# Feature-product weight operands made on GpSimd from blocks loaded once, the x operand made earlier, feature rows stored in pairs

## The chip, the cores and the metric

The kernel runs on one core of a Trainium2 chip. A core has a matrix engine (PE, with its own weight-load stream PEld), VectorE (DVE), ScalarE (ACT), GpSimd (POOL) and a sync engine (SP) that here issues nearly all DMAs, in program order, on one queue. The time is device time in microseconds; lower is better. All arithmetic is on 32-bit floats; a product of full precision is made from three matmuls on operands split into a high part (rounded to the matrix format `R`) and a low remainder.

## The reference

```python
def reference(A_x, A_wqkv, A_wo, ..., B_dft_seq_re, B_dft_seq_im, B_dft_hid_re, B_dft_hid_im, gate_w):
    x = A_x                                        # 1 x 2048 x 640
    g = sigmoid((x * gate_w).sum(-1, keepdims=True))
    q, k, v = split_heads(x @ A_wqkv)              # 32 heads of 20
    p = softmax(einsum("bhqd,bhkd->bhqk", q, k) * 20 ** -0.5)
    a = merge_heads(einsum("bhqk,bhkd->bhqd", p, v)) @ A_wo
    fa, fb = x @ B_dft_hid_re.T, x @ B_dft_hid_im.T   # features
    b = B_dft_seq_re @ fa - B_dft_seq_im @ fb
    return g * a + (1 - g) * b
```

## The kernel before

The work is one hand-ordered program; each engine gets its instructions in the order in which the Python code emits them.

**Projections.** First x is split and the first Q and K columns are made; then V in two halves of 320 columns (`v_pair`, two row tiles a call; each call first fills a V tile with ones on GpSimd, and two V tiles take turns). Then come 32 tiles of the remaining Q and K columns (`qk_pairs`, counted m = 0 to 31): 30 matmuls of 512 columns into two PSUM banks, ScalarE copies one bank out, VectorE adds the other, ScalarE rounds the sum and GpSimd subtracts to get the low part, and SP stores both to `qk_scr`. The low part of every later weight block `wt[c]` is also made on GpSimd (`fin`). Between the tiles PE makes the first score maxima (`run_s`): two steps a tile for m = 2 to 15, one for the others.

**Weight operands.** The features x @ W use a seven-product scheme (`FEATURE`): each product multiplies a sum or difference of two quarter blocks of x by a sum or difference of two quarter blocks of the DFT matrix. There are 14 sets of weight operands (7 products, 2 halves `hf`; 10 of the 14 have two terms). During the tiles `load_set(k)` loads the one or two blocks of a set (409,600 bytes each) into a `wide` tile, of which there are two; GpSimd adds (even m), ScalarE rounds, GpSimd subtracts (odd m), and SP stores the result to `w_scr` and then loads the next set over the same tile.

**Feature stage.** From m = 27 on `load_left(0)` makes the x operand of product 0, and `load_right` brings the stored weight sets back, 1.6 MB each. Then 56 cycles follow, c = 0 to 55, one feature unit u = c (`hid_pair`) in each, interleaved by the string `ORDER` with four steps of attention: scores (`L1052`), exponentials, the maxima of a coming head pair (`L191`) and, at the end of each cycle, a burst of 16 products with V (`L701`). An attention unit is 32 steps, or 8 cycles. A unit's maxima are transposed, stored to `m_scr` and loaded into rows of the q tile (`L240`); the scores of the next unit wait for them.

**Feature rows.** Each unit makes 2 x 128 rows of 320 columns. Rows that an earlier product has begun are added to. Those of products 2 and 4 (u = 16 to 23 and 32 to 39) are in DRAM (`a_scr`): `L489` loads them into one of three slots when the unit starts, GpSimd adds (`L509`), and they are stored eight steps after the unit ends. The fourth load of a product takes the slot of the first, and so waits until that slot's store has landed; SP waits with it, and so does all that follows on SP. Functions given to `at_step(i, ...)` are emitted at the start of attention step i; a unit u starts in step 4u + 1 and ends in step 4u + 3.

**After it** come the products along the sequence (seven products again, `dft_step`, `L782`), interleaved with attention in the same way until the end; `load_a` reads `a_scr` there.

## Time and profile before

| | us |
|---|---|
| median of 3 runs | 1894.74 (1892.43 to 1897.32) |
| the profiled execution | 1897.29 |
| its span | 1895.5 |
| PE busy | 1853.7 (98%) |
| DVE busy | 1453.8 (77%) |
| ACT busy | 1248.2 (66%) |
| POOL busy | 1293.3 (68%) |
| the 32 Q and K tiles | about 106 to 239 |
| the feature stage | about 239 to 607 |

Times in the profile count from the span's start. "A <- B" behind an idle time says that engine A was released by B. SPq is SP's queue of DMA issues. The granted clock (PEclk) is the share of its full rate that PE was given. A row of stretches ("A:B") gives the length, then each engine's busy time, the granted clock, the share of the DMA engines' time and the rate in GB/s.

### The profile page before, as it was taken

Reading aid. Unit: us, or ns where it says so; the run is one execution under the profiler, and the core shown is the slowest. Engines: PE = TensorE matmul, PEld = TensorE weight load, DVE = VectorE, ACT = ScalarE, POOL = GpSimd, SP = SyncE. Lnnn points to the kernel's source line nnn. Section 1 sums busy time; section 2 is a strip of 40 time slices with the busy share of each in tenths; the row PEclk is TensorE's granted clock in tenths of the full one; section 3 lists DMA queues with packets and bytes.
Section 4 is the critical chain, followed back from the end, with each engine's and each line's share of the span. In section 5 each row is a group of like instructions: output and inputs, shape, how many; then the busy total and the mean of one; then the engine's idle time right before and its main releaser. Section 6 shows DMA issues by size and latency. Waiting matters only on the chain. (4 is left out here: it accounts for less than half of the span.)

```text
span 1895.5 us, 45927 instructions
## 1 busy us (share of the span) xinstructions
PE 1853.7 (98%) x17917; PEld 1340.8 (71%) x17917; DVE 1453.8 (77%) x2420; ACT 1248.2 (66%) x2392; POOL 1293.3 (68%) x1092
## 2 busy tenths in 40 slices
PE   9999889989899999999999999999999999999998
PEld 8987657767566677777777777676767676766666
DVE  4156368878778888888888888888888888889953
ACT  4234357767567676767676767676767676777785
POOL 1267653465665999566688989968869988734444
PEclk9999989999999999999999999999999999999999
DMA  7769895677778676544657586747476756533214
GB/s 231 181 230 315 294 264 159 158 214 196 188 199 221 200 215 204 155 122 127 196 162 240 172 236 186 207 133 206 152 209 212 204 170 193 164 86 93 62 48 158
DMA packets 205820, 348.81 MB, mean 184 GB/s; under 512 B 54319, under 2 KB 124079, under 8 KB 205603
## 3 DMA queue, kind: packets, MB, share of 16 engines
q1 hardware_dynamic: 204643, 343.91, 62.3%
q0 software_dynamic: 960, 1.97, 0.6%
q8 instruction: 141, 2.31, 0.5%
q14 instruction: 76, 0.62, 0.1%
HBM read 264.34 MB, written 81.28 MB: 182 GB/s over the span
## 5 line engine op out<-in xcount | busy, mean ns | idle before, releaser
L193 DVE TENSOR_REDUCE mx<-ps 128x1 f32<-128x512 f32 x2048 | 1299.6, 685 | 255.1 <-PE ps L191 214.8
L1058 ACT ACTIVATE p<-ps 128x512 f32<-128x512 f32 x2048 | 1088.0, 598 | 456.8 <-PE ps L191 220.0
L191 PE MATMUL ps<-kst,qst 60*128 60x512 f32 x2048 | 781.4, 414 | 6.9 <-DVE mx L193 4.9
L1052 PE MATMUL ps<-qst,kst 62*128 62x512 f32 x2048 | 698.1, 416 | 13.1 <-DMA qst<-m_scr 13.1
L782 PE MATMUL yp<-x,part 64*128 64x320 f32 x5376 | 643.6, 306 | 0.0
L782 PEld LDWEIGHTS yp<-x,part 64*128 64x128 f32 x5376 | 581.4, 186 | 7.3
L1052 PEld LDWEIGHTS ps<-qst,kst 62*128 62x128 f32 x2048 | 334.4, 185 | 237.5 <-DVE mx L193 129.6
L701 PE MATMUL av<-p,v 128*21 128x512 f32 x4096 | 495.7, 599 | 0.0
L191 PEld LDWEIGHTS ps<-kst,qst 60*128 60x128 f32 x2048 | 370.8, 185 | 20.8 <-DVE mx L193 5.9
L131 POOL TENSOR_TENSOR part<-raw,part 128x1024 fp32r<-128x1024 f32 (+3 forms) x134 | 296.9, 2216 | 15.0 <-ACT part L128 4.8
L701 PEld LDWEIGHTS av<-p,v 128*21 128x21 f32 x4096 | 95.6, 100 | 209.4 <-issue 208.7
L496 PE MATMUL yp<-wb,x 64*128 64x320 f32 x1680 | 212.6, 312 | 7.7 <-POOL p L131 4.5
L130 POOL CAST part<-raw 128x1024 fp32r<-128x1024 f32 (+2 forms) x127 | 125.0, 984 | 134.1 <-PE yp L782 102.6
L643 POOL TENSOR_TENSOR raw<-raw,raw 128x1024 f32<-128x1024 f32 x78 | 188.0, 2411 | 34.2 <-DMA raw<-in_cdft 24.1
L496 PEld LDWEIGHTS yp<-wb,x 64*128 64x128 f32 x1680 | 183.7, 190 | 11.7 <-POOL p L131 4.8
L509 POOL TENSOR_TENSOR x<-x,raw 128x640 f32<-128x640 f32 x40 | 62.4, 1561 | 39.5 <-DVE raw L506 30.8
L131 POOL TENSOR_TENSOR x<-araw,x 128x320 fp32r<-128x320 f32 x96 | 83.8, 873 | 7.7
L853 PE MATMUL yp<-x,part 64*128 64x320 f32 x720 | 87.5, 309 | 0.0
L870 POOL TENSOR_TENSOR x<-x,m 128x320 f32<-128x320 f32 x30 | 26.2, 873 | 79.1 <-DVE m L865 68.2
L853 PEld LDWEIGHTS yp<-x,part 64*128 64x128 f32 x720 | 75.7, 185 | 2.7
L363 PE MATMUL yp<-x,part 64*128 64x512 f32 x480 | 66.0, 398 | 7.2 <-ACT p L369 6.0
L676 POOL TENSOR_TENSOR araw<-araw 128x320 f32<-128x320 f32 x80 | 69.9, 874 | 1.9 <-DMA araw<-a_scr 1.9
(101 smaller groups left out, 1364.7 us busy)
## 6 DMA issues: line engine op xcount, KB each, us to landing
raw<-in_cdft SPq DMA_DIRECT2D x188, 512.0 KB
araw<-a_scr SPq DMA_DIRECT2D x176, 160.0 KB
wb<-w_scr SPq DMA_DIRECT2D x28, 800.0 KB
qk_scr<-p SPq DMA_DIRECT2D x40, 512.0 KB
kst<-qk_scr SPq DMA_DIRECT2D x90, 160.0 KB
qst<-qk_scr SPq DMA_DIRECT2D x90, 160.0 KB
part<-in_xh SPq DMA_DIRECT2D x22, 512.0 KB
w_scr<-wb SPq DMA_DIRECT2D x14, 800.0 KB
```

The costliest lines, as they stand in the source:

```text
L130: e1.tensor_copy(dst1, src)
L131: e2.tensor_tensor(dst2, src, f32(dst1), op=ALU.subtract)
L191: pe.matmul(ps, q[b : b + KROWS, qt * P : (qt + 1) * P], k[b : b + KROWS, kc * 512 : (kc + 1) * 512], start=True, stop=True)
L193: return lambda: dve.tensor_reduce(mx[n][:, h, qt, kc : kc + 1], ps, axis=AX.X, op=ALU.max)
L496: pe.matmul(ps[z], lefts[n][a][r, d, k * P : k * P + P], rights[2 * n + hf][r, b, d], start=done_ == 0, stop=done_ == 3 * ND - 1)
L643: pool.tensor_tensor(raws[0], raws[0], raws[1], op=ALU.add if PRODUCTS[n][0][1][0] > 0 else ALU.subtract)
L676: pool.tensor_tensor(raws[0], raws[0], raws[1], op=ALU.add if PRODUCTS[n][1][1][0] > 0 else ALU.subtract)
L701: pe.matmul(av[32 * j : 32 * j + DH + 1, :], v[:, kt, h * (DH + 1) : (h + 1) * (DH + 1)], pp[qc][:, h, :], start=kt == 0, stop=kt == NS - 1)
L782: pe.matmul(yp[h][:, :HE], c[r, cz, cs], a[r, az], start=s == 0 and z == 0, stop=s == NS - 1 and z == 2)
L853: pe.matmul(yp[h][:, :HE], o[r, oz, d], wos[d, hf][r, wz], start=d == 0 and z == 0, stop=d == ND - 2 and z == 2)
L1052: pe.matmul(pt, k[b : b + KROWS + 2, kt * P : (kt + 1) * P], q[b : b + KROWS + 2, qc * 512 : (qc + 1) * 512], start=True, stop=True)
L1058: act.activation(pts[n, kt, qc][:, h], pt, AF.Exp, scale=float(DH) ** -0.5)
```

## The change

`load_weights(hf)` loads all four quarter blocks of one half at once, 1.6 MB in one DMA, into one `wide` tile: half 0 after the first call of the second V loop, half 1 after tile 8. `make_set` forms a set from those blocks with GpSimd alone: the sum (if there are two terms), the rounding that ScalarE did, and the subtraction. Three sets of half 0 are made during V, into pairs of `p` tiles; the other 11 go into the quarters of the second `wide` tile, one piece of work in each tile from m = 0 to 7 and from 9 to 22, now ahead of that tile's own low part. The high and the low part of a set are stored by a DMA each. The last tiles run in another order (for each of the four column groups t = 2, 3, 0, 1 the products n = 5, 6, 7), so that the x blocks of t = 2 are free after m = 22; the x operand is made from m = 23 on instead of from m = 28 on, and its loads and the `load_right` calls move up with it. The weight block of n = 7 is now finished after m = 19 and used at m = 22 (before: after m = 21, used at m = 25).

`a_scr` gets a layout in which the two row blocks of a unit lie side by side, so that a partition's row is 2,560 bytes in one piece and not two of 1,280. The load of the old rows is emitted four steps after the unit starts, and their store 11 steps after it ends and not 8. `load_a` and `load_a_early` follow the layout, and the first sequence operand uses a `raw` tile for its fourth block.

```diff
@@ -104,7 +104,7 @@
 
     qk_scr = dram.tile([2, 4, 2 * D, 512], F32, name="qk_scr")
     v_scr = dram.tile([NP, P, NS, VW], F32, name="v_scr")
-    a_scr = dram.tile([2, 2, NS, P, HE], F32, name="a_scr")
+    a_scr = dram.tile([2, 2, 2, 4, P, 2, HE], F32, name="a_scr")
     y_scr = dram.tile([NS, P, D], F32, name="y_scr")
     r_scr = dram.tile([NU, 4, 512], F32, name="r_scr")
     l_scr = dram.tile([NU, 4, 512], F32, name="l_scr")
@@ -322,7 +322,7 @@
 
         return finish
 
-    stores, halves = [], []
+    stores, halves, work_ = [], [], []
 
     def flush(keep=0):
         while len(stores) > keep:
@@ -369,6 +369,8 @@
         act.activation(raw, ps[0], AF.Copy)
         dve.tensor_tensor(raw, raw, ps[1], op=ALU.add)
         st = pair_tile()
+        if work_:
+            work_.pop(0)()
         split(st[:, 0].bitcast(R), st[:, 1].bitcast(R), raw, act, pool)
         store_qk(c, t, st, 1)
 
@@ -395,22 +397,23 @@
         flush(1)
 
 
-    def load_set(k):
-        _, terms, _, _ = FEATURE[k // 2]
-        w = wide.tile([P, 2, ND, BW], R, name="wb", bufs=2).rearrange("p z d c -> p (z d c)")
-        half = RW // 2
-        raws = [f32(w)[:, half * i : half * i + half] for i in range(2)]
-        for raw, (_, dh, ri) in zip(raws, terms):
-            sp.dma_start(raw, wr[ri, dh, k % 2])
-
+    def load_weights(hf):
+        w = f32(wide.tile([P, 2, ND, BW], R, name="wb", bufs=2)).rearrange("p z d c -> p (z d c)")
+        w = w[:, : 2 * RW].rearrange("p (b c) -> p b c", b=4)
+        sp.dma_start(w, wr[hf])
+        blocks_ = {(ri, dh): w[:, 2 * ri + dh] for ri in range(2) for dh in range(2)}
+        return [(2 * n + hf, [blocks_[ri, dh] for _, dh, ri in f[1]], f[1][-1][0]) for n, f in enumerate(FEATURE)]
+
+    def make_set(k, terms, sign, hi, lo):
         def add():
             if len(terms) > 1:
-                pool.tensor_tensor(raws[0], raws[0], raws[1], op=ALU.add if terms[1][0] > 0 else ALU.subtract)
+                pool.tensor_tensor(lo, terms[0], terms[1], op=ALU.add if sign > 0 else ALU.subtract)
 
         def finish():
-            split(w[:, 2 * half : 3 * half], w[:, 3 * half : 4 * half], raws[0], act, pool)
-            stores.append((w_scr[k].rearrange("z r (q c) -> (r q) z c", q=2),
-                           f32(w)[:, 2 * half : 4 * half].rearrange("p (z c) -> p z c", z=2)))
+            whole = lo if len(terms) > 1 else terms[0]
+            split(hi.bitcast(R), lo.bitcast(R), whole, pool, pool)
+            for z, part in enumerate((hi, lo)):
+                stores.append((w_scr[k, z].rearrange("r (q c) -> (r q) c", q=2), part))
 
         return add, finish
 
@@ -477,7 +480,7 @@
         ps = [new_y(z)[:, :HE] for z in range(2)]
         fresh = [(th, ri, hf, k) not in seen for _, th, ri in targets]
         seen.update((th, ri, hf, k) for _, th, ri in targets)
-        rows = [a_scr[ri, hf, th * HT + k : th * HT + HT : 4].rearrange("s p c -> p s c") for _, th, ri in targets]
+        rows = [a_scr[ri, hf, th, k] for _, th, ri in targets]
         olds = []
         for (_, th, ri), new, row in zip(targets, fresh, rows):
             old = None
@@ -486,7 +489,7 @@
             elif not new:
                 old = slots.pop(0)
                 slots.append(old)
-                sp.dma_start(old, row)
+                at_step(now[0] + 4, functools.partial(sp.dma_start, old, row))
             olds.append(old)
         done_ = 0
         for d in range(ND):
@@ -514,7 +517,7 @@
             if not new:
                 extras.append((now[0] + 3, functools.partial(add, sign, old)))
             if th != ri or ri == 0 and n == len(FEATURE) - 2 or ri == 1 and last:
-                at_step(now[0] + (4 if new else 8), functools.partial(sp.dma_start, row, m if new else old))
+                at_step(now[0] + (4 if new else 11), functools.partial(sp.dma_start, row, m if new else old))
         yield
 
     step = 0
@@ -561,37 +564,46 @@
         if s == 6:
             fin()
             fin = load_wqk(order[1], pool)
-        if s == 8:
-            sets = [load_set(0)]
+        if s == 0:
+            sets = load_weights(0)
+        if s in (4, 8, 12):
+            add, finish = make_set(*sets.pop(0), *(pair_tile().rearrange("p z c -> p (z c)")[:, : RW // 2] for _ in range(2)))
+            add(), finish()
         if s == 12:
             fin()
-    sets.append(load_set(1))
+    made_sets = f32(wide.tile([P, 2, ND, BW], R, name="wb", bufs=2)).rearrange("p z d c -> p (z d c)")
+    made_sets = made_sets[:, : 2 * RW].rearrange("p (q c) -> p q c", q=4)
+
+    def queue_sets():
+        for q, args in enumerate(sets):
+            work_.extend(make_set(*args, made_sets[:, q % 2 * 2], made_sets[:, q % 2 * 2 + 1]))
+        sets.clear()
+
+    queue_sets()
     free[0] = range(2, 5)
     fin = load_wqk(order[2], pool)
-    tiles = [(n, t) for n in range(6) for t in range(4)] + [(n, t) for t in (2, 3, 0, 1) for n in (6, 7)]
+    tiles = [(n, t) for n in range(5) for t in range(4)] + [(n, t) for t in (2, 3, 0, 1) for n in (5, 6, 7)]
     slabs = []
     for m, (n, t) in enumerate(tiles):
         qk_pairs(order[n], t, m)
         if m == 8:
             load_v(0)
-        if sets:
-            sets[0][m % 2]()
-            if m % 2:
-                sets.pop(0)
-            elif 2 <= m < 2 * SETS - 2:
-                flush()
-                sets.append(load_set(m // 2 + 1))
-        if n < 6 and t == 1:
+            sets = load_weights(1)
+            queue_sets()
+        if n < 5 and t == 1:
             fin()
             if n + 3 < len(order):
                 fin = load_wqk(order[n + 3], pool)
-        if m == 27:
+        if m == 19:
+            fin()
+        if m == 22:
             slabs = load_left(0, raw_stage)
-        if m in (28, 30):
+        if m in (24, 26):
             flush()
-            load_right((m - 28) // 2)
-        if m >= 27:
+            load_right((m - 24) // 2)
+        if slabs:
             slabs.pop(0)()
+    assert not work_
     free[0] = range(5)
     run_s(LEAD)
     flush()
@@ -648,11 +660,11 @@
     c_raws = []
 
     def load_c_first(g):
-        if not c_raws:
+        if g == 0:
             w = f32(wide.tile([P, 2, ND, BW], R, name="wb", bufs=2)).rearrange("p z d c -> p (z d c)")
-            c_raws.extend(w[:, 1024 * q : 1024 * q + 1024] for q in (0, 1, 2, 0))
+            c_raws.extend(w[:, 1024 * q : 1024 * q + 1024] for q in range(3))
         (_, th, ri), (sign, th2, ri2) = PRODUCTS[0][0]
-        raws = [c_raws.pop(0) for _ in range(2)]
+        raws = [c_raws.pop(0) if c_raws else raw_tile() for _ in range(2)]
         for raw, (half, part) in zip(raws, ((th, ri), (th2, ri2))):
             o = (2 * part + g % 2) * 1024
             sp.dma_start(raw, cdft[half * HT + g // 2, :, o : o + 1024])
@@ -668,7 +680,7 @@
         raws = []
         for _, ri, hf in PRODUCTS[n][1]:
             raws.append(apool[0].tile([P, HE], F32, name="araw", bufs=6))
-            sp.dma_start(raws[-1], a_scr[ri, hf, s])
+            sp.dma_start(raws[-1], a_scr[ri, hf, s // 8, s % 4, :, s // 4 % 2])
 
         def finish():
             a = a_tile(n % 2, s)
@@ -681,7 +693,7 @@
     def load_a_early(s0, s1):
         ((_, ri, hf),) = PRODUCTS[0][1]
         raw = f32(part_tile()).rearrange("p z c -> p (z c)")[:, : (s1 - s0) * HE].rearrange("p (s c) -> p s c", c=HE)
-        sp.dma_start(raw, a_scr[ri, hf, s0:s1].rearrange("s p c -> p s c"))
+        sp.dma_start(raw, a_scr[ri, hf, s0 // 8, :, :, s0 // 4 % 2].rearrange("k p c -> p k c"))
         for s in range(s0, s1):
             early.append((s, raw[:, s - s0]))
 
@@ -1012,7 +1024,7 @@
                 if slabs:
                     slabs.pop(0)()
                 if c in (HID - 9, HID - 7, HID - 5):
-                    for s in {9: (0, 8), 7: (4,), 5: (12,)}[HID - c]:
+                    for s in {9: (8, 0), 7: (4,), 5: (12,)}[HID - c]:
                         load_a_early(s, s + 4)
                 if HID - 8 <= c:
                     at_step(i + 2, make_a_early)
@@ -1197,7 +1209,7 @@
     wqk = w[:, : 2 * D].reshape(ND, P, 2 * ND, P).transpose(2, 1, 0, 3)
     xh = np.asarray(A_x)[0].reshape(2, 2, 512, 2, ND, 64).transpose(0, 3, 1, 5, 4, 2).reshape(2, 2, P, ND * 512)
     wr = np.stack([np.asarray(m) for m in (B_dft_hid_re, B_dft_hid_im)])
-    wr = wr.reshape(2, 2, HE, 2, ND, 64).transpose(0, 3, 1, 5, 4, 2).reshape(2, 2, 2, P, RW // 2)
+    wr = wr.reshape(2, 2, HE, 2, ND, 64).transpose(1, 0, 3, 5, 4, 2).reshape(2, 4, P, RW // 2).transpose(0, 2, 1, 3)
     wb = np.zeros((2, P, ND, BW), w.dtype)
     for hf in range(2):
         wb[hf, :, :, :HE] = w[:, 2 * D + hf * HE : 2 * D + (hf + 1) * HE].reshape(ND, P, HE).transpose(1, 0, 2)
```

SP around tile m = 8, where before sets are loaded over stored ones (`wb` is a `wide` tile, `in_wr` the DFT matrix, `w_scr` the finished sets, `in_wqk` a weight block, `v` the V tile of the first heads). Before, and then the change:

```order
L329 DMA qk_scr<-p 128x2x512
L329 DMA w_scr<-wb 128x2x800
L329 DMA qk_scr<-p 128x2x512
L404 DMA wb<-in_wr 128x800 x2
L300 DMA raw<-in_wqk 128x640
L329 DMA qk_scr<-p 128x2x512
L329 DMA w_scr<-wb 128x2x800
L329 DMA qk_scr<-p 128x2x512
L404 DMA wb<-in_wr 128x800
```

```order
L329 DMA w_scr<-wb 128x800 x2
L329 DMA qk_scr<-p 128x2x512
L559 DMA v<-v_scr 128x672
L403 DMA wb<-in_wr 128x3200
L329 DMA qk_scr<-p 128x2x512
L300 DMA raw<-in_wqk 128x640
L329 DMA qk_scr<-p 128x2x512
L329 DMA w_scr<-wb 128x800 x2
```

Between tiles there is no load of `in_wr` any more but this one; the two stores of a set stand where one stood.

GpSimd in the change from tile 17's weight block (`part_1980`, used from m = 21) past tile 19's (`part_2093`, used from m = 22), with the buffers' numbers; `p` is a tile's own low part:

```order
L131 TENSOR_TENSOR part_1980<-raw_1777,part_1980 128x640
L130 CAST wb_1027<-wb_1505 128x800
L131 TENSOR_TENSOR wb_1027<-wb_1505,wb_1027 128x800
L131 TENSOR_TENSOR p_2027<-p_2024,p_2027 128x512
L410 TENSOR_TENSOR wb_1027<-wb_1505 128x800
L131 TENSOR_TENSOR p_2088<-p_2024,p_2088 128x512
L131 TENSOR_TENSOR part_2093<-raw_1983,part_2093 128x640
L130 CAST wb_1027<-wb_1027 128x800
```

Each tile's `p` now stands behind the set's piece, the rounding (CAST) is new on this engine, and two tiles lie between `part_2093` and its first use, where three lay before.

SP in the feature stage about c = 19 to 22, at the end of product 2 (`part<-a_scr` is a load of old rows, `a_scr<-part` a store, `wb<-w_scr` a weight set of 1.6 MB, `m_scr` and `qst<-m_scr` the maxima, `r_scr` and `rb` the softmax sums). Before, and then the change:

```order
L991 DMA a_scr<-part 128x2x320
L423 DMA wb<-w_scr 64x2x1600 x2
L489 DMA part<-a_scr 128x2x320
L991 DMA a_scr<-part 128x2x320
L724 DMA r_scr<-lc 128x16
L234 DMA m_scr<-m 128x64
L489 DMA part<-a_scr 128x2x320
L991 DMA a_scr<-part 128x2x320
L240 DMA qst_94<-m_scr 1x32x32 x4
L728 DMA rb<-r_scr 32x512 x4
```

```order
L1003 DMA a_scr<-part 128x640
L426 DMA wb<-w_scr 64x2x1600 x2
L1003 DMA part<-a_scr 128x640
L1003 DMA a_scr<-part 128x640
L736 DMA r_scr<-lc 128x16
L1003 DMA part<-a_scr 128x640
L234 DMA m_scr<-m 128x64
L1003 DMA a_scr<-part 128x640
L240 DMA qst_94<-m_scr 1x32x32 x4
L740 DMA rb<-r_scr 32x512 x4
```

The load of old rows that stood behind the store of the maxima now stands ahead of it; the loads and stores here belong to units one earlier than those that stood in the same places.

## The prediction

> **What bounds the kernel now.** I read first the page's strip of 40 slices, since a change to one stage can give back only what PE does not use there.
>
> ```profile
> PE   9999889989899999999999999999999999999998
> PEclk9999989999999999999999999999999999999999
> ```
>
> PE is full except in slices 5, 6, 8 and 10 (190 to 520 us): the last projection tiles and the feature stage. After that the change touches only some reads. Then I asked who released PE between 105 and 560 us.
>
> ```profile
> PE ps L1052 <- DMA qst<-m_scr: 11.8, 2, 6.7
> PE yp L363 <- ACT p L369: 6.0, 3, 4.1
> PE yp L496 <- POOL p L131: 4.5, 1, 4.5
> PE ps L191 <- DVE mx L193: 4.1, 2, 3.5
> PE yp L496 <- DMA wb<-w_scr: 2.9, 1, 2.9
> ```
>
> Columns: total, times, longest. Next the stretches in which these waits fall. A wait costs its idle time and then a stretch at a low clock, so I price a stretch as length minus PE busy, plus (1 - clock) times PE busy.
>
> ```profile
> 192.10:239.10 47.00, 39.80 (x314) 30.99 (x311) 15.60 (x24) 15.51 (x26) 30.33 (x22) 0.96 0.83 296
> 239.10:255.50 16.40, 8.65 (x55) 6.55 (x56) 5.66 (x9) 5.37 (x10) 9.17 (x9) 0.69 1.04 259
> 261.00:286.00 25.00, 23.41 (x231) 16.01 (x229) 20.22 (x36) 16.60 (x34) 15.77 (x15) 1.00 0.90 242
> 286.00:311.00 25.00, 25.00 (x246) 18.21 (x243) 21.38 (x38) 18.22 (x36) 3.19 (x3) 0.93 0.70 207
> 397.00:418.00 21.00, 15.90 (x141) 9.73 (x142) 12.36 (x21) 10.54 (x21) 10.69 (x8) 0.84 0.77 226
> 490.00:500.00 10.00, 6.53 (x49) 4.13 (x48) 4.81 (x10) 3.40 (x8) 6.17 (x5) 0.83 0.68 180
> 511.00:536.00 25.00, 18.31 (x160) 11.56 (x150) 13.39 (x23) 11.76 (x24) 13.97 (x11) 0.80 0.83 238
> ```
>
> Lost: 10.4 us at the start of the feature stage (7.75 + 0.31 x 8.65), 3.4 at 261 to 311, 7.6 at 397, 4.6 at 490, 10.4 at 511. For the tiles the count is more direct: their evictions on ScalarE.
>
> ```profile
> 109.86 0.60 ACT L369 ACTIVATE p<-yp 128x512 f32<-128x512 f32 x1 [3.39 <-PE yp L363]
> 181.49 0.58 ACT L369 ACTIVATE p<-yp 128x512 f32<-128x512 f32 x1
> 192.10 0.60 ACT L369 ACTIVATE p<-ps 128x512 f32<-128x512 f32 x1 [1.63 <-PE ps L363]
> 239.10 0.60 ACT L369 ACTIVATE p<-ps 128x512 f32<-128x512 f32 x1 [0.75 <-PE ps L363]
> L191 PE MATMUL ps<-kst,qst 60*128 60x512 f32 x2048 | 781.4, 414 | 6.9 <-DVE mx L193 4.9
> ```
>
> These are tiles 0, 18, 21 and 31. Tiles 19 to 21 took 3.54 us each; at that pace the last ten would take 35.4, they took 47.0: 11.6 lost. With 0.41 more for the 14 tiles with a second score step, the first 21 come to 80.1, against 82.2: 2.1 lost. All together 50 us can be had.
>
> The cause in the tiles:
>
> ```profile
> SPq L404 <- DMA w_scr<-wb: 47.4, 12, 6.1
> 205.02 0.85 SPq L404 DMA_DIRECT2D wb<-in_wr  x2
> 210.24 1.87 POOL L408 TENSOR_TENSOR wb<-wb 128x800 f32<-128x800 f32 x1 [5.45 <-DMA wb<-in_wr]
> 212.14 0.87 ACT L128 ACTIVATE wb<-wb 128x800 fp32r<-128x800 f32 x1 [7.82 <-POOL wb L408]
> ```
>
> SP cannot load a set before the one in that tile is stored; GpSimd waits for the load, ScalarE for GpSimd, and the eviction of a finished tile stands behind that rounding on ScalarE.
>
> **Part 1, sets from blocks.** The 12 waits of SP (105 to 240 us) go, and 14 roundings leave ScalarE. That engine is then free to evict; its 14 x 0.87 = 12 us were hidden where nothing was late, so I give them no gain of their own. The bytes read fall from 24 blocks of 0.41 MB to 8. GpSimd now carries everything:
>
> ```profile
> L131 POOL TENSOR_TENSOR p<-p 128x512 fp32r<-128x512 f32 x32 | 41.3, 1292 | 17.5 <-ACT p L128 17.4
> L408 POOL TENSOR_TENSOR wb<-wb 128x800 f32<-128x800 f32 x10 | 19.1, 1912 | 19.3 <-DMA wb<-in_wr 18.3 <-issue 1.0
> L131 POOL TENSOR_TENSOR wb<-wb 128x800 fp32r<-128x800 f32 x14 | 26.8, 1911 | 1.3 <-ACT wb L128 1.3
> L131 POOL TENSOR_TENSOR part<-raw,part 128x640 fp32r<-128x640 f32 x8 | 12.6, 1570 | 4.9 <-ACT part L128 4.8
> L130 POOL CAST x<-part 128x512 fp32r<-128x512 f32 x30 | 18.3, 611 | 1.6
> L130 POOL CAST part<-raw 128x1024 fp32r<-128x1024 f32 x110 | 114.2, 1038 | 117.1 <-PE yp L782 102.6 <-PE ps L191 8.1 <-DMA y_scr<-yt 2.3
> ```
>
> A rounding of 800 columns is not in the trace; between 0.61 (512) and 1.04 (1024) a line gives 0.85. The bounds are those two. A two-term set and its two tiles then cost 1.91 + 0.85 + 1.91 + 2 x 1.29 = 7.25, with half a weight block 8.04, against 7.1 to 7.9 of PE: GpSimd is the tighter one until m = 22, and what it falls behind it keeps. It falls behind at m = 9, where it waits for the second 1.6 MB load. That load is issued about 143 (tile 8 ends at 141). The 0.82 MB above arrived 5.2 after their issue; twice that is 5.2 if latency were all and 10.4 in proportion. I take 9.5, since a store and the V tile stand just ahead on the queue: 152.5. From there to the weight block of the seventh product's column group, which tile 22 needs, GpSimd has 4 sums, 5 roundings with subtractions, 11 tiles' low parts and 4 weight blocks: 4 x 1.91 + 5 x 2.76 + 11 x 1.29 + 4 x 1.57 = 42.0, so it is ready at 194.5, while PE could start tile 22 at 190 and needs it 0.5 later. **A new wait of 4 us**, 5 with the low clock. Low parts that are late by 8 to 10 us do not stop the tiles before: a tile's rounding needs the `p` tile whose low part was made two tiles (7 us) ago, and the second pair of banks lets PE run 2 to 3 us on. Gain in the tiles: 2.1 + 11.6 - 5 = 8.7, between 14 (load there by 148) and 4 (at 156).
>
> The Trainium skill, "DMA: Bandwidth & Descriptors", section "Bandwidth", has 1 MB DMAs at 341 GB/s and asks for 1 MiB or more a DMA. By that 1.64 MB would take 4.8 us and, behind the same two transfers, be there at about 149.5, the wait at tile 22 would be about 1, and the time 4 less than forecast. No row of before shows a DMA of this size.
>
> **Part 2, three sets during V.** Each puts 4.7 us (once 2.8) of GpSimd ahead of the fill of a V tile.
>
> ```profile
> 78.66 0.45 ACT L387 ACTIVATE v<-ps 128x320 f32<-128x320 f32 x1 [2.68 <-POOL v L383]
> 101.56 0.44 ACT L387 ACTIVATE v<-ps 128x320 f32<-128x320 f32 x1 [1.66 <-PE ps L136]
> ```
>
> The first evicts a row tile that PE made 13 tiles before the second's. At 2.16 us a tile (0.44 busy and some 1.7 idle between two evictions that wait for PE alone) it was done at 73.5, and its eviction is 5 late. Five banks allow 4 x 2.16 = 8.6. With the load ahead of the stores (2 us) and a set ahead of the fill I get 6.5 late at worst: nothing, with 3 us as the upper bound.
>
> **Part 3, x operand earlier.** Five pieces of 1.9 us on GpSimd lie in tiles 23 to 27 instead of 28 and after, and both weight loads are out by tile 27. So the waits for `POOL p` and `wb<-w_scr` go: of the 16.4 us some 6 remain, **10.4 gained** (8 to 10.4). The transfers no longer pile up with the first loads of the feature stage; of the 3.4 at 261 to 311 (scores that waited for late q rows) I expect 2.9 back, none at worst.
>
> **Part 4, feature rows.** The two waits of 11.8 us on `m_scr` are SP's:
>
> ```profile
> SPq L489 <- DMA a_scr<-part: 31.5, 8, 8.2
> 393.68 0.93 SPq L991 DMA_DIRECT2D a_scr<-part  x1
> 395.17 0.42 SPq L234 DMA_DIRECT2D m_scr<-m  x1
> 403.40 0.37 SPq L489 DMA_DIRECT2D part<-a_scr  x1
> 404.37 2.85 SPq L240 DMA_DIRECT2D qst<-m_scr  x4
> 408.56 0.89 PE L1052 MATMUL ps<-qst,kst 62*128 62x512 f32 x2 [5.10 <-DMA qst<-m_scr]
> ```
>
> A load of old rows stood 8 us for a store that itself stood behind 1.6 MB; the load of the maxima came after, and its data 4.2 after that. In the change store and load of one slot are three steps apart instead of two (1.6 us), and the units here are one earlier, so two transfers of 0.33 MB fewer stand ahead (about 2 us at 226 GB/s). Against this, the store of the maxima is now behind the load that waits, so its landing, 1.5 to 3 us, is added. I put the first wait's 7.6 at 4.5, and the second's 10.4 at 9.5 (there twice the x bytes are in flight). The 4.6 at 490 have another owner:
>
> ```profile
> 493.57 0.25 DVE L721 RECIPROCAL lc<-lc 128x16 f32<-128x16 f32 x1 [3.72 <-DMA lc<-l_scr]
> L509 POOL TENSOR_TENSOR part<-part,raw 128x640 f32<-128x640 f32 x16 | 24.9, 1553 | 39.6 <-DMA part<-a_scr 20.5 <-ACT p L1058 13.4 <-DVE mx L193 2.9
> ```
>
> `lc` has one load fewer ahead: 3.5. The second row is the price of the delay: GpSimd already waits 20.5 us for old rows, and now the load is emitted four steps (6 us) nearer to its addition, the first one behind 3.7 MB (four x blocks and a weight set). Three `raw` tiles cover that, just; I charge 2. Sum: 3.1 + 0.9 + 1.1 - 2 = **3** gained, between 22 (all waits gone) and -8. Rows of 2,560 bytes change nothing that I can read from the trace.
>
> **Sum.** 8.7 + 10.4 + 2.9 + 3 = 25. The profiled execution took 1897.3 (span 1895.5); the median is 1894.7. Taken from the median: **1870**.
>
> **Rivals.** (a) All waits go, the load arriving by 148 and SP never standing: 50 less, about 1848. For it: each wait has SP at its root. Against: the slots are still three. (b) The feature rows give back 8: about 1880. For it: the 20.5 us above. (c) The change does not do what it says, as GpSimd takes the place of SP: if a rounding costs as much as a subtraction (1.91), the 11 in the tiles add 1.06 each, 12 in all, all of it on a GpSimd that is already the tighter engine; with (b) 25 - 12 - 11 = 2 are left, about 1893. Against: 1.04 for 1024 columns. (d) Slower: in products 2 and 4 SP's round of store, landing, load exceeds a cycle of 6.25 us. It decides from the point where a landing takes longer than that; if every one of the ten reused slots took the 8.2 seen plus 1.9 of issues, 3.9 are lost each (8.2 + 1.9 - 6.25), 39 in all, against the 22 that the other parts gain: 17 more, about 1911. Against: the mean wait was 3.9.
>
> **Chances.** Forecast 0.52 (its own range 1862 to 1878), (a) 0.13, (b) 0.16, (c) 0.08, (d) 0.11. About 0.3%, 6 us, is what a measurement can tell: faster 0.81, same 0.08, slower 0.11. Eight in ten: 1852 to 1890, with half of (a) left out, and (d).
>
> **What would show it.** Right: no idle of ScalarE on `wb`, tile 31 evicted near 230 and the first product with V near 237; a PE wait of about 4 at tile 22, on a GpSimd `part`; waits on `m_scr` of 2 to 6 near 380 and 495. Wrong: PE idle before 106; a wait on `POOL part` over 10; `raw` or `mx` holding PE in products 2 and 4; more PE idle in the feature stage than the 17 us of before.

## The result, and the profile after

| | before | after |
|---|---|---|
| median, runs side by side | 1898.30 us (1892.43 to 1909.73) | 1886.07 us (1883.91 to 1893.02) |
| ratio after / before, 95% interval | | 0.9938 (0.9912 to 0.9963) |
| the profiled execution, its span | 1897.29, 1895.5 | 1893.02, 1890.9 |

The change makes the kernel 12 us (0.6%) faster. Forecast were 25. The profiled execution of after is the slowest of its runs; it has two late stops of its own (5.6 us near 613 and 3.7 near 1207), the first of which was nearly gone (1.3) when the same kernel was profiled again.

The strip of the page answers to the one that opens the prediction:

```profile
PE   9999899989799999999999999999999999999998
PEclk9999999999899999999999999999999999999999
```

Counted from one, the sixth slice (236 to 284 us) is full now; the fifth, the ninth and the eleventh are not, and the dip of the clock has moved from the sixth to the eleventh. The waits of PE between 105 and 560 us, as before: total, times, longest.

```profile
PE ps L1064 <- DMA qst<-m_scr: 13.0, 2, 7.3
PE ps L191 <- DMA qk_scr<-p: 6.0, 1, 6.0
PE ps L191 <- DVE mx L193: 2.2, 1, 2.2
PE yp L363 <- POOL part L131: 1.1, 1, 1.1
```

The wait of the tiles for ScalarE's evictions is down from 6.0 to 0.6; those for GpSimd's `p` (4.5) and for `wb<-w_scr` (2.9) are gone. The wait on `m_scr` stands as it stood (11.8). A wait on the landing of a store of `p` is new. Now the stretches: length, busy time of PE, PEld, DVE, ACT and POOL, granted clock, DMA share, GB/s.

```profile
40.00:106.00 66.00, 66.00 (x433) 64.56 (x431) 5.72 (x6) 16.27 (x49) 29.06 (x34) 1.00 0.78 201
...
150.00:190.00 40.00, 40.00 (x354) 32.47 (x352) 27.40 (x46) 14.84 (x24) 38.35 (x28) 1.00 0.71 262
...
216.00:220.00 4.00, 4.00 (x38) 4.00 (x36) 2.34 (x4) 1.23 (x2) 3.92 (x5) 1.00 1.02 220
228.00:232.00 4.00, 2.62 (x22) 1.80 (x18) 0.69 (x1) 0.37 (x1) 1.26 (x1) 1.00 1.01 210
...
230.40:236.40 6.00, 0.22 (x1) 0.00 (x0) 0.00 (x0) 0.96 (x2) 0.26 (x1) 0.91 1.00 314
236.40:246.00 9.60, 9.40 (x53) 8.25 (x57) 6.69 (x11) 5.19 (x11) 2.29 (x2) 0.52 0.77 259
250.00:490.00 240.00, 232.13 (x2296) 162.11 (x2296) 203.52 (x350) 168.94 (x335) 128.94 (x107) 0.98 0.69 182
```

V and the tiles up to 190 us are full. Then come 5.8 us of nothing from 230.4 on and 9.6 us at half the clock: by the prediction's price (length less busy, plus (1 - clock) times busy) 5.8 + 0.2 + 4.5 = 10.5 us lost, where before 10.4 were lost. Read also the last column of the two rows at 216 and 228: the DMA engines are busy all the time, and move 210 to 220 GB/s. The row of before from 192 to 239 us has 296 at a share of only 0.83.

Where the stop comes from shows in the timeline, first ScalarE and then SP's issues (start, duration, and in brackets the idle time ahead with its releaser).

```profile
224.78 0.63 ACT L128 ACTIVATE p<-p 128x512 fp32r<-128x512 f32 x1 [5.76 <-DMA qk_scr<-p]
...
227.78 0.58 ACT L369 ACTIVATE p<-yp 128x512 f32<-128x512 f32 x1
235.44 0.63 ACT L128 ACTIVATE p<-p 128x512 fp32r<-128x512 f32 x1 [7.07 <-DMA qk_scr<-p]
235.97 0.58 ACT L369 ACTIVATE p<-ps 128x512 f32<-128x512 f32 x1
```

```profile
212.02 1.37 SPq L426 DMA_DIRECT2D wb<-w_scr  x2
...
214.80 3.56 SPq L329 DMA_DIRECT2D qk_scr<-p  x2
218.45 1.24 SPq L426 DMA_DIRECT2D wb<-w_scr  x2
221.18 18.54 SPq L329 DMA_DIRECT2D qk_scr<-p  x5
```

Tile 30 is evicted at 227.78, against 235.72 before: the tiles are 8 us ahead. Tile 31, for which the prediction named 230, follows only at 235.97 (239.10 before). ScalarE's rounding of a tile (`L128`) writes a `p` tile whose last store must have landed, there are five such tiles, and two right operands of 1.6 MB (`L426`) stand ahead of the stores on SP's queue. ScalarE waits 5.76 us behind the first operand and 7.07 behind the second, and the second time PE runs out of banks. The first product with V comes at 245.8, not at 237.

### The profile page after: what moved, and what is told of

It reads as the page before. It is cut to its first block, busy times and chain, and to the rows that moved or that the text cites. A ratio compares the mean times of both kernels' runs of the same rounds, so it can differ in the third digit from the quotient of the medians.

```text
span 1890.9 us, 45912 instructions
## 1 busy us (share of the span) xinstructions
PE 1853.7 (98%) x17917; PEld 1343.0 (71%) x17917; DVE 1455.3 (77%) x2420; ACT 1237.0 (65%) x2378; POOL 1304.7 (69%) x1106
## 5 line engine op out<-in xcount | busy, mean ns | idle before, releaser
L193 DVE TENSOR_REDUCE mx<-ps 128x1 f32<-128x512 f32 x2048 | 1299.9, 685 | 245.8 <-PE ps L191 219.7
L191 PE MATMUL ps<-kst,qst 60*128 60x512 f32 x2048 | 780.6, 415 | 10.4 <-DMA qk_scr<-p 6.0
L191 PEld LDWEIGHTS ps<-kst,qst 60*128 60x128 f32 x2048 | 369.9, 185 | 23.8 <-ACT p L369 6.4
L131 POOL TENSOR_TENSOR part<-raw,part 128x1024 fp32r<-128x1024 f32 (+3 forms) x134 | 297.0, 2216 | 11.3 <-ACT part L128 1.1
```

The lines of the kernel that those rows point to most:

```text
L131: e2.tensor_tensor(dst2, src, f32(dst1), op=ALU.subtract)
L191: pe.matmul(ps, q[b : b + KROWS, qt * P : (qt + 1) * P], k[b : b + KROWS, kc * 512 : (kc + 1) * 512], start=True, stop=True)
L193: return lambda: dve.tensor_reduce(mx[n][:, h, qt, kc : kc + 1], ps, axis=AX.X, op=ALU.max)
```

## The experiments

Ratios are to the kernel before, run beside each. Of each profile I give the start of the first product with V (one such product begins each cycle), by how much some cycles were longer than the usual 6.25 us each, and PE's waits on `m_scr`, in us. Five of the kernels (after, same_again, the two maxima runs, rows_old) do the same up to that first product, which comes at 244.3 to 246.5: differences of 2 us in that column are noise.

| kernel | ratio (95% interval) | first product with V | cycle 4 | 22-23 | 35-36 | 38-39 | `m_scr` |
|---|---|---|---|---|---|---|---|
| before | 1 | 255.5 | 3.5 | 7.1 | 4.9 | 9.4 | 11.8 |
| after | 0.9938 (0.9912, 0.9963) | 245.8 | 0 | 7.8 | 4.1 | 10.4 | 13.0 |
| same_again | 0.9929 (0.9910, 0.9949) | 246.5 | 0 | 8.1 | 5.1 | 9.4 | 12.6 |
| right_late | 0.9940 (0.9919, 0.9960) | 238.2 | 8.6 | 9.6 | 4.4 | 8.6 | 14.3 |
| both_late | 0.9925 (0.9904, 0.9945) | 237.5 | 4.7 | 10.0 | 5.3 | 10.1 | 15.5 |
| right_wide | 1.1492 (1.1465, 1.1519) | 293.5 | 0 | 32.2 | 27.9 | 33.2 | 82.4 |
| right_queues | 0.9929 (0.9907, 0.9951) | 242.4 | 0 | 8.5 | 2.9 | 9.9 | 13.1 |
| right_twice | 0.9852 (0.9828, 0.9875) | 250.0 | 0 | 0 | 0 | 5.1 | 3.3 |
| some_twice | 0.9869 (0.9846, 0.9892) | 242.0 | 0 | 4.0 | 0 | 5.1 | 5.3 |
| twice_late | 0.9847 (0.9825, 0.9868) | 248.8 | 4.5 | 0 | 0 | 0.9 | 0.6 |
| before_twice | 1.0046 (1.0029, 1.0062) | 285.0 | 0 | 0 | 0 | 3.3 | 2.9 |
| maxima_pool | 0.9952 (0.9935, 0.9970) | 244.3 | 0 | 11.0 | 4.5 | 11.0 | 17.6 |
| maxima_act | 1.0069 (1.0044, 1.0094) | 244.3 | 0 | see below | | | 0 |
| rows_old | 0.9929 (0.9909, 0.9949) | 244.3 | 0 | 8.8 | 2.8 | 7.9 | 11.8 |

**same_again**, the changed kernel once more.

> The changed kernel once more, so that the others have it on the same chip. Theory: the four long stops of its first trace (PE idle 6 us near 231 us, some 8 us of lost cycle time near 390, 4 near 470 and 10 near 500) come from the order of its transfers and repeat within 2 us each; the two at 613 us (5.6 over the usual cycle) and 1207 us (3.7) do not have to. Time 1884 to 1890. Rival: the stops are chance and sit elsewhere in this trace.

Measured 1886.92 us. The stops at 231, 22-23, 35-36 and 38-39 repeat to within 1.1 us; the one at 613 us is down to 1.3. So the four have to be explained.

**right_late and both_late: the order on SP's queue.**

```diff
-        if m in (24, 26):
+        if m == 24:
             flush()
-            load_right((m - 24) // 2)
+            load_right(0)
...
     flush()
+    load_right(1)
# both_late also:
-                if k == 0 and n + 1 < len(FEATURE):
+                if k == (2 if n == 0 else 0) and n + 1 < len(FEATURE):
```

> Only the load of the second right operand (1.6 MB) moves from tile 26 to behind the last tile. Theory (store queue): the stores of the last p tiles landed late because they stood behind that load; ScalarE's 7.07 us wait for qk_scr<-p near 235 us goes, so do PE's 6.0 and the low clock behind it; the first product with V comes near 237 instead of 245.8; 6 to 10 us less than the changed kernel, less where up to 3.5 come back in cycle 4 as scores that wait for late q rows. Rival (GpSimd): those stores were late because GpSimd made the low parts late; the stop stays within 2 us and so does the time.

> right_late, and the first pieces of the second product's x operand (1 MB) are asked for two cycles later (cycle 2 instead of 0), behind the stacks of the next pair of heads. In right_late PE's stop near 231 us was gone (first product with V at 238.2) but cycle 4 took 14.9 us instead of 6.2, as scores waited 6.3 us for q rows. Theory (too many bytes at once): each megabyte ahead of the q rows on the queue is worth some 3 to 4 us there; the first product with V stays near 238, cycle 4 falls to 10 or less, 4 to 8 us less than the changed kernel (ratio to before 0.989 to 0.991). Rival (the second right operand alone is late): cycle 4 stays above 13 and the time is that of right_late.

PE's waits in right_late, then in both_late:

```profile
PE ps L1065 <- DMA qst<-m_scr: 14.3, 2, 7.4
PE ps L191 <- DMA qst<-qk_scr: 6.3, 1, 6.3
```

```profile
PE ps L1065 <- DMA qst<-m_scr: 15.5, 2, 7.9
...
PE ps L191 <- DMA qst<-qk_scr: 2.7, 1, 2.7
```

The cause of the stop at 231 is shown: with the second operand behind the tiles, it is gone, and the first product with V comes 7.6 us earlier. The load on the queue made it, not GpSimd. But the time is the same (1888.26): cycle 4 loses 8.6 us, because the q rows of the next heads are now behind that operand. With 1 MB of x taken out of the way as well, half of this comes back, and the time falls to 1882.32, at a ratio whose interval overlaps that of the changed kernel. So what one place gives, the other takes. I read this as too many microseconds of transfer between 200 and 265 us, wherever the loads stand; the next runs make the transfers shorter.

**right_wide, right_queues, right_twice: how long a right operand takes.** Between 216 and 220 us an operand's load was nearly alone, with the engines full at 220 GB/s. It goes to 64 partitions, then to the other 64. Three ways of writing to all 128 at once:

```diff
# right_wide
-        for h in range(2):
-            sp.dma_start(f32(w)[64 * h : 64 * h + 64], w_scr[k].rearrange("z r c -> r z c"))
+        for z in range(2):
+            sp.dma_start(f32(w)[:, z], w_scr[k, z : z + 1].to_broadcast([2, 64, RW]))
# right_queues
-        for h in range(2):
-            sp.dma_start(f32(w)[64 * h : 64 * h + 64], ...)
+        for h, q in enumerate((sp, pool)):
+            q.dma_start(f32(w)[64 * h : 64 * h + 64], ...)
# right_twice
-    w_scr = dram.tile([SETS, 2, 64, RW], F32, name="w_scr")
+    w_scr = dram.tile([SETS, 2, 2, 64, RW], F32, name="w_scr")
-                stores.append((w_scr[k, z].rearrange("r (q c) -> (r q) c", q=2), part))
+                for h in range(2):
+                    stores.append((w_scr[k, z, h].rearrange("r (q c) -> (r q) c", q=2), part))
+        for z in range(2):
+            sp.dma_start(f32(w)[:, z], w_scr[k, z].rearrange("h r c -> (h r) c"))
```

> All 14 right operands are loaded as two transfers of 128 partitions (high part, low part) instead of two of 64 partitions (both parts); same bytes, same packets of 6400 bytes. Theory (half of the partitions, half of the rate): in the trace such packets took 461 ns where packets of 3200 took 139 and of 4096 took 204, so an operand takes 7.4 us; now 4.7 to 5. The stop near 231 us shrinks from 6 to 3 or less and each wait on m_scr by 2 to 3, together 8 to 14 us less than the changed kernel. Rival (rate set by the reads from DRAM or by the queue's other traffic): packets stay above 400 ns and the time within 2 us.

> The changed kernel with the two halves of each right operand's load issued by SyncE (partitions 0 to 63) and GpSimd (64 to 127); nothing is stored twice. Theory (64 partitions take half the rate, in order on one queue): with both halves in flight at once the packets of 6400 fall towards 250 ns and an operand lands in about 5 us; the stop near 231 us and the waits on m_scr fall as in right_twice, without its doubled stores: ratio to before 0.978 to 0.986. Rival 1: the engines still take one transfer after the other, packets stay at 460 to 490 ns, ratio 0.991 to 0.995. Rival 2: GpSimd waits at the load for PE and its additions come late: above 0.995.

> Every set of right operands is stored twice, so that it can be loaded as two transfers of 128 rows to 128 partitions; loads keep their bytes and packets of 6400, the stores of sets double (0.82 MB more for each of 14 sets, between 70 and 205 us). In right_wide the packets fell from 461 to 251 ns, but a transfer with an outermost step of 2 took some 30 us, as if on 2 of the 16 engines. Theory (64 partitions take half the rate): packets near 250 ns on all 16 engines, an operand lands in 4 to 5 us instead of 7.4; the stop near 231 us and the waits on m_scr shrink by 2 to 3 each: 5 to 12 us less than the changed kernel, less what the doubled stores cost in the tiles (up to 5). Rival: with 16 engines at once the packets go back to 400 ns or more, and the time is that of the changed kernel or longer.

**right_wide** took 285 us more than the kernel before. Its DMA strip from 240 to 262 us:

```profile
DMA  1111111111111111111189611111111111111111
GB/s 47 47 70 47 47 58 58 47 47 70 47 47 45 52 52 48 52 60 58 47 318 416 251 58 58 58 47 47 58 58 47 47 58 58 47 47 58 58 47 47
```

A tenth of the engines' time is busy, at 47 to 58 GB/s: two of 16 engines (2/16 = 0.125). The source's outermost step has two entries, the halves. The Trainium skill, "DMA: Bandwidth & Descriptors", section "Why a DMA increments its semaphore by 16 and not by 1", says that the slowest dimension larger than one sets how many engines share a copy; the strip agrees.

**right_queues** changed nothing that can be measured (1882.33 us). GpSimd's halves took 9.9 us in the median from issue to landing:

```profile
wb<-w_scr POOLq DMA_DIRECT2D x14, 800.0 KB, 9.9
```

**right_twice** is 26 us faster than before, and by the ratios (0.9852 against 0.9929) about 15 faster than the change. Two of PE's waits, and three stretches:

```profile
PE ps L1065 <- DMA qst<-m_scr: 3.3, 1, 3.3
PE ps L191 <- DMA qk_scr<-p: 2.9, 1, 2.9
```

```profile
230.00:240.00 10.00, 8.96 (x70) 6.52 (x66) 1.38 (x2) 2.23 (x4) 6.95 (x6) 1.00 1.01 391
...
378.00:381.00 3.00, 3.00 (x39) 2.99 (x36) 2.94 (x5) 2.88 (x6) 3.00 (x3) 1.00 1.05 429
...
250.00:490.00 240.00, 240.00 (x2416) 168.99 (x2416) 213.70 (x368) 177.32 (x350) 140.12 (x115) 1.00 0.62 200
```

With full engines the DMAs move 391 GB/s from 230 to 240 us, where stores of `p` run beside an operand, and 429 from 378 to 381, where by the trace's records of packets an operand is alone, as it was in after at 216 (220). PE is idle for nothing in 240 us of the feature stage, where after had 7.9 us idle and a clock of 0.98. The operands' packets have 6400 bytes in both kernels; by the same records between 240 and 520 us their median time falls from 494 to 244 ns. So these loads to 64 partitions had half the rate, and kept all 16 engines busy meanwhile. The two kernels also read the rows in another order (high and low part in turn, or one after the other); no run separates that from the number of partitions. The Trainium skill, "SBUF — State Buffer", section "Door 1: The DMA port swizzle", has this rule: partitions 0 to 63 reach 8 of 16 ports, 196 GB/s at 1 MiB against 328 for 128 partitions; and its section "Can I just issue two DMAs to hit both halves?" says no. Both agree with these runs (half the rate here; 462 ns in right_queues, against 494). The price is in the tiles: with the doubled stores the first product with V comes at 250.0.

**some_twice and twice_late**, two cuts of right_twice.

```diff
# some_twice, on right_twice
+FAST = (0, 1, 6, 9, 10)
+                for h in range(1 + (k in FAST)):
+            if k in FAST:
+                sp.dma_start(f32(w)[:, z], w_scr[k, z].rearrange("h r c -> (h r) c"))
+            else:
+                sp.dma_start(f32(w)[64 * z : 64 * z + 64], w_scr[k, :, 0].rearrange("z r c -> r z c"))
```

> As right_twice, but only 5 of the 14 sets are stored twice and loaded as two transfers of 128 partitions: the first two of the feature stage (whose loads stand ahead of the last stores of p) and sets 6, 9 and 10 (loaded near 375, 452 and 489 in the changed kernel, each just ahead of a long stop); the other nine are stored once and loaded as in the changed kernel. Theory (few loads matter: those that stand ahead of a store that a wait hangs on): the first product with V comes near 240 to 243 as fewer stores are doubled, the waits on m_scr stay under 5 together, ratio to before 0.979 to 0.984, below right_twice. Rival (what counts is the sum of time that the queue spends on loads): nine slow loads bring most of the waits back, m_scr above 8, ratio 0.987 to 0.991.

> right_twice with the edits of both_late (second right operand behind the last tile, second x operand two cycles later). In right_twice the first product with V came at 250.0 and the feature stage lost only 5 us. Theory: the last stores of p stood behind the second operand there too; the first product with V comes near 246, and cycle 4 loses less than 2 with loads at the full rate: ratio 0.982 to 0.984. Rival: the doubled stores (150 to 230 us) set the start, and the time stays at 0.985 or, with a stop in cycle 4, goes to 0.987.

some_twice took 1874.06 us, between the two expectations: the start comes 8 us earlier than in right_twice, as its theory had it, but 22-23 loses 4.0 again and `m_scr` 5.3. Its time cannot be told from that of right_twice (the intervals overlap); its cycles say that loads which stand just ahead of a stop carry most of the stop's price, not all. twice_late (1868.08) is the fastest median, and level with right_twice (1869.49) within the intervals: 38-39 gives 4.2 back and cycle 4 takes 4.5.

**maxima_pool, maxima_act, rows_old: the wait on `m_scr`.** In the feature stage the store and the loads of the maxima go out by GpSimd or by ScalarE; rows_old has the old timing of the feature rows:

```diff
# maxima_pool; in maxima_act, act stands for pool
+        q2 = pool if 0 <= now[0] < start else sp
         def store():
-            sp.dma_start(m_scr[n], f32(m))
+            q2.dma_start(m_scr[n], f32(m))
...
-                    sp.dma_start(f32(q[b : b + 1, :]).rearrange(...
+                    q2.dma_start(f32(q[b : b + 1, :]).rearrange(...
# rows_old
-                at_step(now[0] + 4, functools.partial(sp.dma_start, old, row))
+                sp.dma_start(old, row)
-                at_step(now[0] + (4 if new else 11), functools.partial(sp.dma_start, row, m if new else old))
+                at_step(now[0] + (4 if new else 8), functools.partial(sp.dma_start, row, m if new else old))
```

> In the feature stage the store and the four loads of the score maxima are issued by GpSimd instead of SyncE. Theory (order on SyncE): the store of the maxima stood 8.7 us behind a load of old rows that waited; PE's two waits on m_scr, 13.0 together, fall to 4 to 6, with the low clock behind them 8 to 12 us less than the changed kernel. Rival (traffic): the store and loads land late because of the 1.6 MB transfers ahead of them, whoever issues them; the waits stay above 10. Second rival: GpSimd stops for the landing of the store (2 to 4 us) and the rows that it adds come later, PE waits for raw tiles instead, no gain.

> In the feature stage the store and the loads of the score maxima are issued by ScalarE instead of SyncE. With GpSimd as issuer nothing was gained: its own addition, just ahead, waited for the same old rows. ScalarE has no such wait. Theory (order on SyncE): the store goes out within 1 us of its data (near 381 instead of 388) and PE's waits on m_scr (12.6 to 13.0 in the changed kernel) fall to 5 or less, 8 to 12 us less than the changed kernel (ratio 0.986 to 0.989). Rival (traffic): store and loads land as late as before because 1.6 MB are in flight; the waits stay above 10 and the ratio at 0.993. ScalarE's five issues of 0.4 to 0.7 us a unit cost nothing under 6.2 us of PE a cycle.

> The changed kernel with the old timing of the feature rows (load of old rows at the start of a unit, store 8 steps after it instead of 11); the layout in pairs stays. Theory: the new timing gained nothing, since in both the store of the maxima stood 8 us at SyncE because of old rows; time within 3 us of the changed kernel, waits on m_scr 11 to 14. Rival of the prediction's part 4: the new timing gains 3, so this is 3 or more slower. Third: the new timing itself costs, this is 3 or more faster.

First the place itself, SP's issues near cycle 22 in after, and under it in right_twice:

```profile
377.99 1.13 SPq L736 DMA_DIRECT2D r_scr<-lc  x1
387.82 0.32 SPq L1003 DMA_DIRECT2D part<-a_scr  x1
388.23 1.06 SPq L234 DMA_DIRECT2D m_scr<-m  x1
```

```profile
379.11 0.38 SPq L737 DMA_DIRECT2D r_scr<-lc  x1
385.24 0.32 SPq L1004 DMA_DIRECT2D part<-a_scr  x1
385.65 0.38 SPq L234 DMA_DIRECT2D m_scr<-m  x1
```

After `r_scr<-lc` SP stands until the slot's old store has landed, 8.7 us (377.99 + 1.13 to 387.82) in after, 5.8 in right_twice, and the maxima, split at 379, go out behind that load. In right_twice that is still in time: cycles 22-23 lose nothing. The place of the store on SP's queue looks like the cause here; the three runs bear that out only for a small part.

maxima_pool: no gain, 1891.15 us. GpSimd's own order holds the store, behind two additions:

```profile
387.59 1.55 POOL L514 TENSOR_TENSOR part<-part,raw 128x640 f32<-128x640 f32 x1 [3.06 <-DVE mx L193]
...
390.57 0.61 POOL L236 DMA_DIRECT2D m_scr<-m  x1
394.01 2.14 POOL L242 DMA_DIRECT2D qst<-m_scr  x4 [2.83 <-DMA m_scr<-m]
```

maxima_act: 1911.34 us. No wait on `m_scr` is left on PE's list, but it has only changed its owner: PE now waits for ScalarE (`PE ps L191 <- ACT p`, 23.0 us in all), and ScalarE for the maxima. Here around the stop, which lies in cycle 21 now:

```profile
391.16 0.32 ACTq L236 DMA_DIRECT2D m_scr<-m  x1
391.60 2.31 ACT L1072 ACTIVATE p<-ps 128x512 f32<-128x512 f32 x4 [1.02 <-PE ps L191]
399.49 3.31 ACTq L242 DMA_DIRECT2D qst<-m_scr  x4
402.90 1.09 ACT L1072 ACTIVATE p<-ps 128x512 f32<-128x512 f32 x2 [9.00 <-DMA qst<-m_scr]
```

The maxima are ready at 391.1 and their store goes out at once, with nothing ahead of it on ScalarE. Still ScalarE can issue the loads only at 399.49. By the trace's records the store's 128 packets of 256 bytes run from 397.1 to 398.9: until then the engines work at an operand's load, issued at 385.61, and at feature rows. In a quiet place (277.61) the same store had landed after 1.6 us. So cycles 21-22 lose 10.9 us and 37-38 lose 11.3. That is the rival of this run's expectation, traffic. From the maxima to the loads it takes 8.4 us here and 11.8 in after (379.4 to 391.15), so the order on SP made some 3 of them. The second loss is ScalarE's own, in every unit:

```profile
279.71 1.25 ACTq L242 DMA_DIRECT2D qst<-m_scr  x1
279.76 0.59 ACT L1072 ACTIVATE p<-ps 128x512 f32<-128x512 f32 x1
281.00 2.05 ACTq L242 DMA_DIRECT2D qst<-m_scr  x3
283.15 1.08 ACT L1072 ACTIVATE p<-ps 128x512 f32<-128x512 f32 x2 [2.80 <-DMA qst<-m_scr]
```

Four issues take 3.3 us, with no exponential between 280.35 and 283.15, and two cycles of each of the other five units are together 4 us or more too long. The expectation that five issues cost nothing was wrong.

rows_old: 1884.16 us, the ratio of same_again to the last digit. The new timing of the feature rows gains nothing and costs nothing that these intervals, some 4 us to each side, can tell. In this run the store of the maxima stands ahead of the load that waits:

```profile
382.22 0.48 SPq L234 DMA_DIRECT2D m_scr<-m  x1
390.84 0.32 SPq L492 DMA_DIRECT2D part<-a_scr  x1
391.73 2.83 SPq L240 DMA_DIRECT2D qst<-m_scr  x4
```

It goes out 6 us earlier than in after, its packets run from 389.7 to 390.5, and the loads follow at 391.73 (391.15 in after). The order of store and wait changes nothing, as the store's own transfer is as late as the end of SP's wait.

**before_twice**: the loads and stores of right_twice in the kernel before.

```diff
-            stores.append((w_scr[k].rearrange("z r (q c) -> (r q) z c", q=2), ...))
+            for h in range(2):
+                stores.append((w_scr[k, :, h].rearrange("z r (q c) -> (r q) z c", q=2), ...))
```

> The kernel before with every set stored twice and loaded as two transfers of 128 partitions, as in right_twice. It asks how much of the time the change was worth where loads of right operands are no longer slow. Theory: the feature stage gains some 14 as in right_twice (waits on m_scr 11.8 to under 4); the tiles lose, since SyncE waits for each store of a set before the next load and the stores double, by 1 to 2 us for each of 12: ratio 0.995 to 1.005, so that the change is worth 1 to 2 per cent on top (18 to 38 us), against 0.6 to 0.7 as it was made. Rival: the waits of the tiles are hidden, ratio below 0.99, and the change is worth less than 10 us on top.

Measured 1904.90 us. Its feature stage has the gain of right_twice (`m_scr` 2.9, cycles 22 to 36 clean), so that is a matter of the loads and not of the change. Its tiles lose more than I expected:

```profile
SPq L404 <- DMA w_scr<-wb: 66.2, 13, 7.6
```

SP's wait for its own stores rises from 47.4 to 66.2 us, and the first product with V comes at 285.0, against 250.0 in right_twice. All of the 35 us between these two kernels lie before that product: with heavier stores the change is worth much more than the 12 us above. How much of the 35 comes from SP's waits, and how much from the earlier x operand, no run separates.

## Why the prediction was wrong by half

The direction held, and 1886 lies in the wide range (1852 to 1890) but outside the forecast's own (1862 to 1878); the gain was 12 where 25 were forecast. Two steps failed, the first of part 3 and the price of part 4. Step by step:

- **Part 1 came out near its sum, in part by luck.** SP's 12 waits in the tiles are gone. GpSimd's rounding of 800 columns took 0.85, as taken. The second 1.6 MB landed 8.65 us after its issue (142.60 to 151.25; taken: 152.5), the weight block for tile 22 was ready at 192.7 (taken: 194.5), and PE, which came to that tile 1 us later than taken, waited 1.1 and not 4. The estimate that the prediction made from the figure of the Trainium skill ("DMA: Bandwidth & Descriptors", section "Bandwidth") had this wait right (about 1), but the landing too early (149.5). Tile 30 is evicted 7.9 us earlier than before; 8.7 were forecast for tile 31. As the wait was some 3 us shorter than charged, as much went elsewhere in the last ten tiles, where ScalarE already waits for stores of `p` (4.0 us ahead of tile 22's eviction at 197.26): two errors of nearly the same size cancelled.

```profile
151.25 1.91 POOL L410 TENSOR_TENSOR wb<-wb 128x800 f32<-128x800 f32 x1 [6.65 <-DMA wb<-in_wr]
...
191.15 1.53 POOL L131 TENSOR_TENSOR part<-raw,part 128x640 fp32r<-128x640 f32 x1
```

- **Part 2 was right.** PE is busy for 66.0 of 66.0 us from 40 to 106, as before.
- **Part 3 failed at its first step.** "Of the 16.4 us some 6 remain, 10.4 gained": the two waits named there did go, but the same loads, four to five tiles earlier, stood ahead of the last stores of `p`, and 10.5 us were lost in a stop that the prediction did not look for. Tile 31 is evicted at 235.97 and not near 230, and the first product with V comes at 245.8 and not near 237. The step had asked what waits for the loads, and not what waits behind them on the queue. right_late shows this, and right_twice why it costs so much. The second step, 2.9 back at 261 to 311, was right: cycle 4 has no stop (3.5 gained). But right_late shows that the two are one budget: what one place gives, the other takes.
- **Part 4 failed at "I put the first wait's 7.6 at 4.5".** The stretches that were to give 3 gave nothing: 7.1 + 4.9 + 9.4 = 21.4 before, 7.8 + 4.1 + 10.4 = 22.3 after, 22.6 in same_again. Three steps more and two transfers fewer were to shorten SP's wait for a slot; its waits are 31.5 us in 8 before and 33.8 in 8 after. And the step took the wait on `m_scr` for SP's alone. In before, the store of the maxima, issued at 395.17, landed by the trace's records of packets only at 403.07, and SP went on at 403.40: the maxima would have been late without SP's wait too. Both stand behind operands at half the rate; in right_twice, with nothing changed in the order, the same store landed 2.6 us after its issue, and these waits fall from 13.0 to 3.3. The 2 us charged for late old rows do not show: GpSimd's wait for them grew from 20.5 to 48.8 us, and PE's list above names none for them.
- **The sum.** The start gained 9.7 of the 19.1 in the first two terms, cycle 4 gave 3.5, the feature rows took 0.9: 12.3, as in the medians. Against the forecast that is 9.4 less at the start, 3.9 less in the feature rows and 0.6 more in cycle 4.
- **The rivals.** (d) did not come: the waits for slots took 33.8 us in 8, at most 9.4, and neither `raw` nor `mx` held PE for more than 2.2. (c) fell with the rounding of 0.85. The time of (b), 1880, lies nearest to the result, but not for its reason: the feature rows took 0.9, not 8. (a) came in no run here; the fastest has 1868. The likeliest rival, slow transfers that move from one stop to the next, was not on the list, though its sign was in the rows quoted: 259 GB/s at a DMA share of 1.04 from 239 to 255 us, against 296 at 0.83 in the tiles. The prediction took such a number (226) as a rate and did not ask why it was low.

Left open: what the tiles would give if operands could be had at the full rate without doubled stores, and why 5.1 us are still lost at 38-39 in right_twice (3.3 of them a wait on `m_scr`), of which twice_late has 0.9. Neither was tried.

## What to carry to other kernels

When a load is moved forward on an in-order queue, list the stores behind it and who needs their tiles back: here five `p` tiles turned a late store into a stop of the matrix engine. Where DMA engines are full, compare GB/s between stretches first; here a low rate at a full share came from transfers to 64 partitions, and no order of the queue mended it. Before you put a late small transfer down to its place in a queue, see when its own packets ran. If moving a transfer moves the stop by as much, count the microseconds of transfer in the whole stretch, not the waits.

## What the runs showed of the hardware

- Loads of operands to 64 partitions ran at 210 to 220 GB/s with all engines busy (after, 216 to 220 and 228 to 232 us), loads of the same size to 128 partitions at 429 (right_twice, 378 to 381); issuing the halves from two engines at once did not help (packets' median 462 ns against 494, and 244 over 128 partitions).
- A store of 32 KB that was issued while an operand was loading landed 8.3 us after its issue by SP (rows_old, 382.22 to 390.5) and 7.7 after its issue by ScalarE (maxima_act, 391.16 to 398.9), against 1.6 in a quiet place (277.61): another engine's queue did not take it past the transfers in flight.
- A copy whose source has an outermost step of two entries kept a tenth of the engines' time busy, at 47 to 58 GB/s; 28 such transfers made the kernel 285 us slower than before.
- Four small loads issued by ScalarE held it for 3.3 us, more than the exponentials could spare in a cycle of 6.25 us.
